# Attention pipeline on three shared PSUM banks, with the sums for the Strassen products of x and h moved from VectorE to GpSimd

## The chip, the cores and the metric

One core of a Trainium2 chip. The metric is the device time of one execution in microseconds (us), as the median of several runs. Engines: TensorE (PE in the profile, and PEld for its loading of weights), VectorE (DVE), ScalarE (ACT), GpSimd (POOL), and the queue that starts DMAs (SP).

## The reference

A transformer block on 2048 tokens of width 1024: a layer norm, linear attention with 32 heads of 32, a residual, a second layer norm, a gated ReLU MLP of width 3584, and a second residual.

```python
phi = lambda t: jnp.where(t > 0, t + 1, jnp.exp(t)) + 1e-6
pq, pk = phi(q), phi(k)
kv = jnp.einsum("bhsd,bhse->bhde", pk, v)
z = jnp.einsum("bhsd->bhd", pk)
num = jnp.einsum("bhqd,bhde->bhqe", pq, kv)
den = jnp.einsum("bhqd,bhd->bhq", pq, z)[..., None] + 1e-6
# ... o = num / den, put together again, times wo ...
h = x + _A_ref(_layernorm(x, axis=-1), A_wqkv, A_wo)
h2 = h + _B_ref(_layernorm(h, axis=-1), B_W_gate, B_W_up, B_W_down)
```

## The kernel before

The large products are made with Strassen's scheme in Winograd's form: seven products of quarters instead of eight, at the price of sums of quarters on both sides. The left sums are four additions or subtractions for each piece of the transposed, normalized x (`xT`) or h (`hnT`), all on VectorE. One of them is written over a quarter of its own input.

```python
def left_sums(T, S, cols):
    (a11, a12), (a21, a22) = [[v[:, :, cols] for v in row] for row in blocks(T)]
    s1, s2, s4 = (v[:, :, cols] for v in S)
    nc.vector.tensor_tensor(out=s1, in0=a21, in1=a22, op=ALU.add)
    nc.vector.tensor_tensor(out=s2, in0=s1, in1=a11, op=ALU.subtract)
    nc.vector.tensor_tensor(out=a21.bitcast(FP16), in0=a11, in1=a21, op=ALU.subtract)
    nc.vector.tensor_tensor(out=s4, in0=a12, in1=s2, op=ALU.subtract)
```

x is taken in four units of four tiles (128 tokens each). Unit 0 makes k and v with plain products, while units 1 to 3 are normalized, transposed and summed ahead of their Strassen products. Four x sums of 128x1024 belong to each unit.

```python
def ln_T(t):                                   # layer norm of a tile of x, then its transpose
    # ... bn_stats, bn_aggr on VectorE, ln and exp on ScalarE ...
    nc.vector.scalar_tensor_tensor(out=nmr, in0=mv[:, 0:1], scalar=-1.0, in1=rstd, op0=ALU.mult, op1=ALU.mult)
    nc.scalar.activation(out=xn[:], in_=x_sb[:], func=ACT.Identity, bias=nmr, scale=rstd)
    # ... DMA transpose into xT ...

def phi_end(dst, e):
    nc.scalar.activation(out=e, in_=dst, func=ACT.Exp, bias=negb[:, 0:1], scale=1.0)
    nc.vector.tensor_scalar(out=e, in0=e, scalar1=1.0, scalar2=PHI_EPS, op0=ALU.min, op1=ALU.add)
    nc.vector.tensor_tensor(out=dst, in0=dst, in1=e, op=ALU.max)

# ... in the loop over units: k products, kv of the unit before, v products ...
            for n, _ in enumerate(v_unit(u)):
                if n == 1 and u + 1 < NU:
                    sums_unit(u + 1)
        sums_unit(0)
```

In `strassen` ScalarE copies a product out of its bank (`snap`, tiles `m` and `u`), so that the next product may go on in that bank. VectorE evicts the finished products (`phi_begin` for k and q; the `v_sb` additions for v).

In the attention stage every tile passes four steps, each one step later than the one before: numerator and denominator (`nd`, one PSUM bank), the DMA transpose of the result (`oT`), the product with wo in two halves (`attn`, two other banks) with the layer norm of h, and the transpose of normalized h. The MLP's first products ("quads") fill TensorE in between. The sums of h are made in one piece of 128x2048 at the end of each half.

```python
abpool = abctx.enter_context(tc.tile_pool(name="abpool", bufs=2, space=PSUM, side="right"))
# ...
ndpool = abctx.enter_context(tc.tile_pool(name="ndpool", bufs=1, space=PSUM, side="right"))
# ...
LAG = (0, 1, 2, 3)
STS = ST // NS
QSTEPS = STS + 2
def attn_step(step):
    for k in range(4):
        n = step - LAG[k]
        if n in begin_at:
            n = begin_at.index(n)
            stages[n][k]()
            if k == 3 and (n + 1) % STS == 0:
                left_sums(hnT[n // STS], hns[n // STS], slice(0, SW))
```

Of the kernel before, what the change touches and what calls it, by code (L numbers as in the profile page):

```python
# [8 lines left out]
ALU = mybir.AluOpType  # L9
FP32 = mybir.dt.float32  # L10
BF16 = mybir.dt.bfloat16
FP16 = mybir.dt.float16
PSUM = bass.MemoryType.PSUM
# [18 lines left out]
def block_kernel(ctx: ExitStack, tc: tile.TileContext, x, wqkv, wo, wg, wu, wd, out, H: int):  # L32
    nc = tc.nc
    P = 128
    xf = x.flatten_outer_dims()
    of = out.flatten_outer_dims()
    S, D = xf.shape
# [4 lines left out]
    KC = D // P  # L42
    FC = F // P
    NW = 512
    NDW = P + HPC
    SW = 512
# [4 lines left out]
    NT = SW // P  # L51
# [20 lines left out]
    hh_dram = [[dram.tile([P, FH, SW], BF16, name=f"hh_dram{s}_{q}") for q in range(4)] for s in range(NS)]  # L72

    PE_T = 4
    XB, HB = 4, 2
    negb = consts.tile([P, 2], FP32, name="negb")
    nc.gpsimd.memset(negb[:, 0:1], -1.0 - PHI_EPS)
    nc.gpsimd.memset(negb[:, 1:2], 1.0 + PHI_EPS)
# [9 lines left out]
    bwork = pqctx.enter_context(tc.tile_pool(name="bwork", bufs=2, side="right"))  # L88
# [9 lines left out]
    xT, xS = [None] * NS, [None] * NS  # L98
# [5 lines left out]
    def blocks(T):  # L104
        return [[T[i][:, j * KH:(j + 1) * KH, :] for j in range(2)] for i in range(2)]

    def left_sums(T, S, cols):

        (a11, a12), (a21, a22) = [[v[:, :, cols] for v in row] for row in blocks(T)]
        s1, s2, s4 = (v[:, :, cols] for v in S)  # L110
        nc.vector.tensor_tensor(out=s1, in0=a21, in1=a22, op=ALU.add)
        nc.vector.tensor_tensor(out=s2, in0=s1, in1=a11, op=ALU.subtract)
        nc.vector.tensor_tensor(out=a21.bitcast(FP16), in0=a11, in1=a21, op=ALU.subtract)
        nc.vector.tensor_tensor(out=s4, in0=a12, in1=s2, op=ALU.subtract)

    def left_ops(T, S):
        (a11, a12), (a21, a22) = blocks(T)
# [83 lines left out]
    with ExitStack() as actx:  # L201
# [9 lines left out]
        x_tiles = {}  # L211

        def load_x(t):
            x_sb = bwork.tile([P, D], BF16, tag="x_res", bufs=XB, name="x_sb")
            nc.sync.dma_start(out=x_sb[:], in_=xf[t * P:(t + 1) * P, :])
            x_tiles[t] = x_sb

# [3 lines left out]
        def place(t):  # L221
            i, r = divmod(t * P, HS)
            s, r = divmod(r, SW)
            return s, i, r
# [3 lines left out]
        atiles = [t for u in units for t in u]  # L228
# [121 lines left out]

        def sums_unit(u):
            s, _, r = place(units[u][0])
            left_sums(xT[s], xS[s], slice(r, r + 2 * P))

        NU = len(units)

# [7 lines left out]
        for n, t in enumerate(units[0]):  # L364
            v_plain(t)
            if todo:
                ln_T(todo.pop(0))
            if n == 1:
                sums_unit(1)
                k_sums()  # L370
# [21 lines left out]
        for c in range(KC):  # L392
            bnk, i = divmod(c, GPB)
            nc.vector.tensor_tensor(out=kvz[:, c, :], in0=kv_ps[bnk][:, i * NDW:(i + 1) * NDW],
                                    in1=mask[:], op=ALU.mult)


    abctx = ExitStack()
    abpool = abctx.enter_context(tc.tile_pool(name="abpool", bufs=2, space=PSUM, side="right"))
    qw = []  # L400

    def q_unit(s, c):
# [26 lines left out]


    mctx = ExitStack()
    ndpool = abctx.enter_context(tc.tile_pool(name="ndpool", bufs=1, space=PSUM, side="right"))

    hnT, hns = [], []

# [24 lines left out]
    def attn_stages(t):  # L460

        i, r = divmod(t * P, HS)
        s, r = divmod(r, SW)
        st = {}

        def nd():
            o_sb = bwork.tile([P, D], BF16, tag="o_sb", name="o_sb")
            st["o"] = o_sb
            ov = o_sb[:].rearrange("p (k h e) -> p k h e", k=KC, h=HPC)
            for c0, n in pieces:  # L470
                ps = ndpool.tile([P, NW], FP32, tag="nd", name="nd")
                for c in range(c0, c0 + n):
                    nc.tensor.matmul(ps[:, (c - c0) * NDW:(c - c0 + 1) * NDW], lhsT=pqT[:, c, t * P:(t + 1) * P],
                                     rhs=kvz[:, c, :], start=True, stop=True)
                ndv = ps[:, 0:n * NDW].rearrange("p (k w) -> p k w", w=NDW)
                den = bsmall.tile([P, GPB, HPC], FP32, tag="den", name="den")
                nc.scalar.activation(out=den[:, 0:n], in_=ndv[:, :, P:NDW], func=ACT.Identity, bias=deps[:], scale=1.0)
                rd = bsmall.tile([P, GPB, HPC], FP32, tag="rd", name="rd")
                nc.vector.reciprocal(out=rd[:, 0:n], in_=den[:, 0:n])
                nc.vector.tensor_tensor(  # L480
                    out=ov[:, c0:c0 + n], in0=ndv[:, :, 0:P].rearrange("p k (h e) -> p k h e", h=HPC),
                    in1=rd[:, 0:n, :].unsqueeze(3).to_broadcast([P, n, HPC, Dh]), op=ALU.mult)

        def oT():
            st["oT"] = bwork.tile([P, KC, P], BF16, tag="oT", name="oT")
            nc.sync.dma_start_transpose(out=st["oT"][:], in_=st["o"][:])
            x_sb = bwork.tile([P, D], BF16, tag="x_res", bufs=XB, name="x_res")
            nc.sync.dma_start(out=x_sb[:], in_=xf[t * P:(t + 1) * P, :])
            st["x"] = x_sb

        def wo_h():
            h_sb = st["x"]
            tot = bsmall.tile([P, 2], FP32, tag="tot", name="tot")
            for j in range(2):
                ps = abpool.tile([P, NW], FP32, tag="ab", name="attn")
                for c in range(KC):
                    nc.tensor.matmul(ps[:], lhsT=st["oT"][:, c, :], rhs=wo_sb[:, c, j * NW:(j + 1) * NW],  # L497
                                     start=(c == 0), stop=(c == KC - 1))
                nc.vector.scalar_tensor_tensor(out=h_sb[:, j * NW:(j + 1) * NW], in0=ps[:], scalar=1.0,  # L499
                                               in1=h_sb[:, j * NW:(j + 1) * NW], op0=ALU.mult, op1=ALU.add,  # L500
                                               accum_out=tot[:, j:j + 1])
            nc.sync.dma_start(out=h_dram[t][:], in_=h_sb[:])
            st["hn"] = bwork.tile([P, D], BF16, tag="hn", bufs=HB, name="hn")

            sm = bsmall.tile([P, 6], FP32, tag="sm", name="sm")
            nmean, var, lnv, rstd, nmr = (sm[:, i:i + 1] for i in range(5))
            nc.vector.tensor_tensor(out=nmean, in0=tot[:, 0:1], in1=tot[:, 1:2], op=ALU.add)
            nc.vector.tensor_scalar(out=nmean, in0=nmean, scalar1=-1.0 / D, scalar2=None, op0=ALU.mult)
            nc.scalar.activation(out=st["hn"][:], in_=h_sb[:], func=ACT.Square, bias=nmean, scale=1.0, accum_out=var)
            nc.scalar.activation(out=lnv, in_=var, func=ACT.Ln, bias=LN_EPS, scale=1.0 / D)  # L510
            nc.scalar.activation(out=rstd, in_=lnv, func=ACT.Exp, scale=-0.5)
            nc.vector.tensor_tensor(out=nmr, in0=nmean, in1=rstd, op=ALU.mult)
            nc.scalar.activation(out=st["hn"][:], in_=h_sb[:], func=ACT.Identity, bias=nmr, scale=rstd)

        def hn_T():
            nc.sync.dma_start_transpose(out=hnT[s][i][:, :, r:r + P], in_=st["hn"][:])

        return nd, oT, wo_h, hn_T

    LAG = (0, 1, 2, 3)  # L520
    STS = ST // NS
    QSTEPS = STS + 2
    stages = [attn_stages(t) for t in order]
    begin_at = [n if n < STS else n - STS + QSTEPS for n in range(ST)]

    def attn_step(step):
        for k in range(4):
            n = step - LAG[k]
            if n in begin_at:
                n = begin_at.index(n)  # L530
                stages[n][k]()
                if k == 3 and (n + 1) % STS == 0:
                    left_sums(hnT[n // STS], hns[n // STS], slice(0, SW))

    rest = [p for s in range(1, NS) for c in range(0, KH, 2) for p in [q_unit(s, c)] * 6]
    for step in range(QSTEPS):
        attn_step(step)
        for p in rest[step * len(rest) // QSTEPS:(step + 1) * len(rest) // QSTEPS]:
            next(p)
# [123 lines left out]
    for f in range(NE):  # L663
        st = {}
# [3 lines left out]
            next(st["q"])  # L668

        flow += [begin] + [lambda st=st: next(st["q"])] * 5  # L670
    ready = STS + LAG[3]
    for step in range(QSTEPS, ready):
        if step == QSTEPS:
            flow.pop(0)()
        attn_step(step)
    steps = QSTEPS + STS + LAG[3] - ready
    for n in range(steps):
        attn_step(ready + n)
        for p in flow[n * len(flow) // steps:(n + 1) * len(flow) // steps]:
# [13 lines left out]
    prev, k = None, 1  # L693
# [129 lines left out]
@with_exitstack  # L823
def kernel(
    ctx: ExitStack,
    tc: tile.TileContext,
    A_x: bass.AP,
    A_wqkv: bass.AP,
    A_wo: bass.AP,
    B_x: bass.AP,  # L830
    B_W_gate: bass.AP,
    B_W_up: bass.AP,
    B_W_down: bass.AP,
    out: bass.AP,
):
    block_kernel(tc, A_x, A_wqkv, A_wo, B_W_gate, B_W_up, B_W_down, out, H=32)
# [30 lines left out]
```

## Time and profile before

776.76 us, median of 3 runs (773.99 to 778.0). The profiled run has a span of 773.6 us at a mean granted TensorE clock of 0.996.

The first part of the page gives the busy time of every engine, its share of the span and its instructions.

```profile
PE 742.8 (96%) x3584; PEld 337.9 (44%) x3584; DVE 490.0 (63%) x924; ACT 313.6 (41%) x529; POOL 3.5 (0%) x34
```

TensorE is the limit and GpSimd does nothing. The table of windows cuts the span at events of TensorE. The columns are the window, its length, the busy time (and instructions) of PE, PEld, DVE, ACT and POOL, the granted clock, the share of DMA and GB/s. The first row shown is from the first Strassen product of k to that of the second unit; the second is from the first quad to the first wide quad (where attention is over).

```profile
40.62:70.53 29.91, 26.86 (x145) 12.80 (x144) 29.21 (x56) 23.26 (x39) 0.50 (x4) 1.00 0.59 127
...
208.58:301.44 92.86, 88.30 (x433) 39.50 (x432) 69.31 (x200) 52.83 (x114) 0.00 (x0) 0.96 0.54 124
```

In the first of these VectorE is busy for 29.21 of 29.91 us. It is the crowded place that the change wants to relieve. The waits of TensorE (total, times, longest) name what is lost to whom:

```profile
PE attn L497 <- DMA oT<-o_sb: 5.8, 7, 2.5
...
PE Aq L276 <- ACT v_sb L329: 1.1, 1, 1.1
...
PE Aq L276 <- ACT m L143: 0.7, 2, 0.5
```

### The profile page before, as it was taken

The numbers are of one execution on the slowest core, as the hardware profiler recorded it, in microseconds if no ns is written. First come the engines' busy times: TensorE is split into PE (matmuls) and PEld (weight loads), VectorE is DVE, ScalarE is ACT, GpSimd is POOL, SyncE is SP. The second block draws the span as 40 slices with busy tenths as digits, with TensorE's granted clock in tenths as the row PEclk, the third lists the DMA queues.
The fourth block names the chain that finished last, engine by engine and source line by source line (L and its number), as shares of the span: only waits on it lengthen the run. The fifth ranks groups of instructions, "written<-read, shape, count | busy, mean of one in ns | idle before, by whom it ended". The sixth has DMA issues, their size and how long they took to land.

```text
span 773.6 us, 9575 instructions
## 1 busy us (share of the span) xinstructions
PE 742.8 (96%) x3584; PEld 337.9 (44%) x3584; DVE 490.0 (63%) x924; ACT 313.6 (41%) x529; POOL 3.5 (0%) x34
## 2 busy tenths in 40 slices
PE   5989999989979998999999999999999999999998
PEld 2444555434434443444444444444443444444443
DVE  6998545876878767675464654646554991349732
ACT  4775554856836654444444444444443000000000
POOL 0000000000000000000000000000000000000000
PEclk9999999999989999999999999999999999999999
DMA  9863003097656545354014040140001985971001
GB/s 311 235 134 82 0 1 109 2 244 175 154 108 149 137 109 144 116 157 136 7 37 121 28 136 8 34 123 28 27 8 40 310 283 193 308 286 48 28 27 55
DMA packets 125150, 89.76 MB, mean 116 GB/s; under 512 B 50352, under 2 KB 116912, under 8 KB 124592
## 3 DMA queue, kind: packets, MB, share of 16 engines
q1 hardware_dynamic: 125104, 89.15, 40.6%
q8 instruction: 28, 0.46, 0.2%
q14 instruction: 18, 0.15, 0.1%
HBM read 59.77 MB, written 17.83 MB: 100 GB/s over the span
## 4 chain that ended last, share of the span: by engine, by line
PE 44%; DVE 11%; ACT 3%; issue 2%; DMA 1%; DVEq 0%
PE A L576 15%; PE accA L737 10%; PE E L576 8%; PE accE L737 6%; DVE gu L595 4%; PE Dp L576 3%; ACT snap L590 2%; PE accD L737 2%; DVE hh L598 1%; DMA out_dram<-o 1%; ACT gu L597 1%; DVE hh L651 1%; DVE tg L559 1%; DVE tu L556 1%; DVE tg L556 1%
## 5 line engine op out<-in xcount | busy, mean ns | idle before, releaser
L595 DVE TENSOR_TENSOR gu<-E,snap 128x1024 bf16<-128x1024 f32 x48 | 58.7, 1222 | 88.1 <-ACT snap L590 85.5
L590 ACT COPY snap<-A 128x1024 f32<-128x1024 f32 x72 | 72.0, 1008 | 85.6 <-PE A L576 85.6
L737 PEld LDWEIGHTS <-hh 128*128 128x128 bf16 (+1 forms) x560 | 54.7, 98 | 67.7 <-issue 1.9
L597 ACT ACTIVATE gu<-gu 128x512 bf16<-128x512 bf16 x72 | 45.4, 630 | 86.7 <-DVE gu L595 86.4
L737 PE MATMUL accA<-wd,hh 128*128 128x512 f16 (+1 forms) x336 | 73.3, 379 | 1.4 <-DVE gu L595 1.4
L497 PE MATMUL attn<-wo_mem,oT 128*128 128x512 bf16 x256 | 62.9, 388 | 5.8 <-DMA oT<-o_sb 5.8
L576 PEld LDWEIGHTS <-tg 128*128 128x128 f16 x384 | 37.5, 98 | 50.8 <-issue 6.8
L576 PEld LDWEIGHTS <-tu 128*128 128x128 f16 x384 | 37.6, 98 | 45.3
L598 DVE TENSOR_TENSOR hh<-gu 128x512 bf16<-128x512 bf16 x72 | 30.4, 423 | 38.1 <-ACT gu L597 38.1
L576 PE MATMUL A<-hn,tg 128*128 128x512 f16 (+1 forms) x192 | 49.3, 379 | 1.1 <-ACT snap L590 1.1
L576 PE MATMUL A<-hn,tu 128*128 128x512 f16 (+1 forms) x192 | 49.3, 379 | 0.0
L143 ACT COPY u<-Aq 128x512 f32<-128x512 f32 x56 | 32.0, 581 | 29.2 <-PE Aq L276 19.1
L576 PEld LDWEIGHTS <-wg 128*128 128x128 bf16 x288 | 28.1, 98 | 35.6 <-issue 2.4
L576 PEld LDWEIGHTS <-wu 128*128 128x128 bf16 x288 | 28.2, 98 | 34.0
L497 PEld LDWEIGHTS <-oT 128*128 128x128 bf16 x256 | 24.1, 99 | 32.7 <-DMA oT<-o_sb 8.4
L737 PEld LDWEIGHTS <-s 128*128 128x128 f16 x224 | 21.9, 98 | 27.2 <-issue 0.8
L595 DVE TENSOR_TENSOR gu<-Dp,snap 128x1024 bf16<-128x1024 f32 x24 | 29.3, 1219 | 1.9 <-PE Dp L576 1.9
L276 PEld LDWEIGHTS <-xT 128*128 128x128 bf16 (+1 forms) x192 | 18.6, 98 | 24.8 <-issue 3.1
L745 DVE TENSOR_TENSOR u<-accA,hres 128x512 f32<-128x512 f32 x16 | 10.7, 687 | 28.4 <-PE accA L737 27.9
L480 DVE TENSOR_TENSOR o_sb<-nd,rd 128x384 bf16<-128x384 f32 (+1 forms) x48 | 24.5, 510 | 4.3 <-DMA oT<-o_sb 2.1
L499 DVE SCALAR_TENSOR_TENSOR x_res<-attn,x_res 128x512 bf16<-128x512 f32 x32 | 21.9, 684 | 7.0 <-PE attn L497 6.6
L576 PE MATMUL A<-hs,tg 128*128 128x512 f16 x96 | 24.6, 379 | 1.1 <-ACT snap L590 1.1
(159 smaller groups left out, 1216.8 us busy)
## 6 DMA issues: line engine op xcount, KB each, us to landing
wd<-in_B_W_down_dram SPq DMA_DIRECT2D x16, 896.0 KB, 6.9
hh_dram<-hh SPq DMA_DIRECT2D x72, 128.0 KB, 1.7
wg<-in_B_W_gate_dram SPq DMA_DIRECT2D x14, 512.0 KB, 5.1
wu<-in_B_W_up_dram SPq DMA_DIRECT2D x14, 512.0 KB, 6.1
hh<-hh_dram SPq DMA_DIRECT2D x4, 1792.0 KB, 8.8
x_sb<-in_A_x_dram SPq DMA_DIRECT2D x16, 256.0 KB, 3.2
x_res<-in_A_x_dram SPq DMA_DIRECT2D x16, 256.0 KB, 2.9
h_dram<-x_res SPq DMA_DIRECT2D x16, 256.0 KB, 2.4
```

The lines of the kernel that those rows point to most:

```text
L143: nc.scalar.copy(out=snaps[nm, v], in_=A[v][:])
L276: nc.tensor.matmul(ps[:], lhsT=left[m - 1][:, kc, r + v * P:r + (v + 1) * P], rhs=right[m - 1][:, kc, :], start=(start and kc == 0), stop= ...
L480: nc.vector.tensor_tensor(out=ov[:, c0:c0 + n], in0=ndv[:, :, 0:P].rearrange("p k (h e) -> p k h e", h=HPC), in1=rd[:, 0:n, :].unsqueeze(3 ...
L497: nc.tensor.matmul(ps[:], lhsT=st["oT"][:, c, :], rhs=wo_sb[:, c, j * NW:(j + 1) * NW], start=(c == 0), stop=(c == KC - 1))
L499: nc.vector.scalar_tensor_tensor(out=h_sb[:, j * NW:(j + 1) * NW], in0=ps[:], scalar=1.0, in1=h_sb[:, j * NW:(j + 1) * NW], op0=ALU.mult, ...
L556: nc.vector.tensor_tensor(out=t[:, 0], in0=b[0][1], in1=b[0][0], op=ALU.subtract)
L576: nc.tensor.matmul(ps[:, v, :], lhsT=w[v][m - 1][:, kc, :], rhs=left[m - 1][:, kc, :], start=(start and kc == 0), stop=(kc == KH - 1), ski ...
L590: nc.scalar.copy(out=m[:], in_=ps[:])
L595: nc.vector.tensor_tensor(out=gu[:], in0=ps[:], in1=m[:], op=ALU.add)
L597: nc.scalar.activation(out=gu[:, 0, :], in_=gu[:, 0, :], func=ACT.Relu)
L598: nc.vector.tensor_tensor(out=d, in0=gu[:, 0, :], in1=gu[:, 1, :], op=ALU.mult)
L737: nc.tensor.matmul(accs[tt][:], lhsT=lhs[:, half * FD + f, tt * P:(tt + 1) * P], rhs=rhs[half][:, f, :], start=(start and half == 0 and f ...
```

## The change

Two things are done at once. The attention stage gets one pool of three banks for `nd` and `attn` together, three buffers for `oT`, other lags and two steps fewer before the second half starts; the sums of h are made in slices of one tile. And the left sums of x and of h go to GpSimd, to take 20.7 us of work off VectorE (16 sums of 0.68 us and 8 of 1.22 us).

```diff
-    def left_sums(T, S, cols):
+    def left_sums(T, S, cols, eng):
-        nc.vector.tensor_tensor(out=s1, in0=a21, in1=a22, op=ALU.add)
+        eng.tensor_tensor(out=s1, in0=a21, in1=a22, op=ALU.add)
 (... the other three sums likewise ...)
-            left_sums(xT[s], xS[s], slice(r, r + 2 * P))
+            left_sums(xT[s], xS[s], slice(r, r + 2 * P), nc.gpsimd)
-    abpool = abctx.enter_context(tc.tile_pool(name="abpool", bufs=2, space=PSUM, side="right"))
+    abpool = abctx.enter_context(tc.tile_pool(name="abpool", bufs=3, space=PSUM, side="right"))
-    ndpool = abctx.enter_context(tc.tile_pool(name="ndpool", bufs=1, space=PSUM, side="right"))
+    ndpool = abpool
 (... x tiles: three buffers of each of two tags, was four of one; oT shares one of these tags; x is read again in a stage of its own, x_in ...)
-    LAG = (0, 1, 2, 3)
+    LAG = (0, 1, 1, 2, 4)
-    QSTEPS = STS + 2
+    QSTEPS = STS + 0
-                if k == 3 and (n + 1) % STS == 0:
-                    left_sums(hnT[n // STS], hns[n // STS], slice(0, SW))
+                if k == len(LAG) - 1 and n % STS >= NT:
+                    left_sums(hnT[n // STS], hns[n // STS], slice(n % NT * P, (n % NT + 1) * P), nc.gpsimd)
```

More of the change, by code (lines that the diff above doesn't have):

```diff
@@ L74, in block_kernel @@
     PE_T = 4
-    XB, HB = 4, 2
+    XB, HB = 3, 2
     negb = consts.tile([P, 2], FP32, name="negb")
@@ L105, in blocks @@
         return [[T[i][:, j * KH:(j + 1) * KH, :] for j in range(2)] for i in range(2)]
-    def left_sums(T, S, cols):
+    def left_sums(T, S, cols, eng):
         (a11, a12), (a21, a22) = [[v[:, :, cols] for v in row] for row in blocks(T)]
         s1, s2, s4 = (v[:, :, cols] for v in S)
-        nc.vector.tensor_tensor(out=s1, in0=a21, in1=a22, op=ALU.add)
-        nc.vector.tensor_tensor(out=s2, in0=s1, in1=a11, op=ALU.subtract)
-        nc.vector.tensor_tensor(out=a21.bitcast(FP16), in0=a11, in1=a21, op=ALU.subtract)
-        nc.vector.tensor_tensor(out=s4, in0=a12, in1=s2, op=ALU.subtract)
+        eng.tensor_tensor(out=s1, in0=a21, in1=a22, op=ALU.add)
+        eng.tensor_tensor(out=s2, in0=s1, in1=a11, op=ALU.subtract)
+        eng.tensor_tensor(out=a21.bitcast(FP16), in0=a11, in1=a21, op=ALU.subtract)
+        eng.tensor_tensor(out=s4, in0=a12, in1=s2, op=ALU.subtract)
     def left_ops(T, S):
@@ L213, in load_x @@
         def load_x(t):
-            x_sb = bwork.tile([P, D], BF16, tag="x_res", bufs=XB, name="x_sb")
+            x_sb = bwork.tile([P, D], BF16, tag=("x_res", "oT")[atiles.index(t) % 2], bufs=XB, name="x_sb")
             nc.sync.dma_start(out=x_sb[:], in_=xf[t * P:(t + 1) * P, :])
@@ L470, in nd @@
             for c0, n in pieces:
-                ps = ndpool.tile([P, NW], FP32, tag="nd", name="nd")
+                ps = ndpool.tile([P, NW], FP32, tag="ab", name="nd")
                 for c in range(c0, c0 + n):
@@ L484, in oT, with x_in @@
         def oT():
-            st["oT"] = bwork.tile([P, KC, P], BF16, tag="oT", name="oT")
-            nc.sync.dma_start_transpose(out=st["oT"][:], in_=st["o"][:])
+            oT = bwork.tile([P, D], BF16, tag="oT", bufs=XB, name="oT")
+            st["oT"] = oT[:].rearrange("p (c t) -> p c t", c=KC)
+            nc.sync.dma_start_transpose(out=st["oT"], in_=st["o"][:])
+        def x_in():
             x_sb = bwork.tile([P, D], BF16, tag="x_res", bufs=XB, name="x_res")
@@ L516, in hn_T @@
             nc.sync.dma_start_transpose(out=hnT[s][i][:, :, r:r + P], in_=st["hn"][:])
-        return nd, oT, wo_h, hn_T
-    LAG = (0, 1, 2, 3)
+        return nd, oT, x_in, wo_h, hn_T
+    LAG = (0, 1, 1, 2, 4)
     STS = ST // NS
-    QSTEPS = STS + 2
+    QSTEPS = STS + 0
     stages = [attn_stages(t) for t in order]
@@ L526, in attn_step @@
     def attn_step(step):
-        for k in range(4):
+        for k in range(len(LAG)):
             n = step - LAG[k]
@@ L670, in block_kernel @@
         flow += [begin] + [lambda st=st: next(st["q"])] * 5
-    ready = STS + LAG[3]
+    ready = STS + LAG[-1]
     for step in range(QSTEPS, ready):
@@ L675, in block_kernel @@
         attn_step(step)
-    steps = QSTEPS + STS + LAG[3] - ready
+    steps = QSTEPS + STS + LAG[-1] - ready
     for n in range(steps):
```

## The prediction

> **What bounds the kernel now.** TensorE. The page's busy table gives PE 742.8 of 773.6 us (96%). Counting matmuls at their spacing in the timeline (0.216 us for 512 columns, 0.058 for 132) the work is about 728 us, so about 45 us of the span is not matmul issue. From about 305 us the chain of waits is TensorE with small vector pieces, and the change doesn't touch that code. What can be won lies before 305 us. By the busy table in 10-us windows, TensorE is idle there 23 us: about 8.5 at the start, 3 between 40 and 70 us, 9.5 between 150 and 230 us, 2 at 300-310 us. Between 220 and 230 us the granted clock is also only 0.66, after 2.6 idle us in the window before; that costs 2-3 us more. Named waits in the attention stage (waits of PE): oT transposes 5.8 us, Dq on vector evictions 2.4 us, nd on its single bank 1.0 us; weight loads for nd waited 11.8 us for o_sb. VectorE is 90-100% busy from 10 to 70 us and 66-98% from 150 to 220 us.
>
> **What the change does.** The counts of TensorE work stay the same. nd and attn share three banks instead of one plus two; oT has three buffers; the second half starts two steps earlier (20 steps, not 21); a tile's nd matmuls and its 16 attn matmuls now stand together in the order. Hn transposes come one step later. VectorE loses 16 sums of 128x1024 (0.68 us each, 10.9 us) and 8 of 128x2048 (1.22 us each, 9.8 us). GpSimd gets 16 of 128x1024 and 32 of 128x512. The trace has no such GpSimd operation; the Trainium skill, "GPSIMD Engine Reference", Performance versus the Vector engine, gives about 2.6 cycles per element, so my estimate is 2.2 and 1.2 us: about 36 us for x, 38 us for h.
>
> The cost: "SBUF — State Buffer", Who interferes with whom, says a GpSimd instruction that reads SBUF and a vector instruction with two SBUF inputs lock each other out whole. The weight sums (1.2 us each; tv around 35-45 us, tq around 52-60 us) and the phi maximum fall in the same stretches, so a vector instruction will wait up to 2.2 us, and the evictions queued behind it too.
>
> **On the critical path.**
> - 40-70 us: the kv matmuls move into a hole, but tv sums collide with the sums of unit 1; S2 still arrives near 42-44 us. Loss 3 us becomes 3-7: +2.
> - 150-230 us: fewer bank waits and fewer steps, -5; the clock dip may vanish, -2; against it, in the pure-attention steps the first attn bank waits for nd's eviction (1.2 us), and the first S2 product waits for the late transpose plus two GpSimd sums (about 3 us, as large as the wait that VectorE makes now): +2. The oT wait behind the gate/up loads (2.5 us) stays.
> - 300-310 us: the sums of h are sliced and early, -1.
>
> Sum: -4 us.
>
> **Predicted: 772.5 us, 80% range 763 to 782.** Faster by over 2%: 0.08; within 2%: 0.83; slower by over 2%: 0.09.
>
> **What would show it.** GpSimd busy near 75-80 us; sums of 2.2 and 1.2 us; vector two-input sums stretched over 1.22 and 0.68 us at 35-75 us; TensorE idle of 150-230 us down from 9.5 to about 5 us; nd waits for o_sb gone; the windows after 310 us unchanged in length.
>
> **What would make it wrong.** If GpSimd and VectorE hardly block each other, or the attention stage gets nearly gapless at full clock: 760-765 us. If blocked vector evictions stall TensorE through 40-75 us and again beside the h sums, or the late h sums hold the first quads: 780-790 us.

## More of the kernel before

Last, some groups of VectorE instructions up to 306 us (line, operation, output from input, shapes, count; then busy us and the mean ns of one; then idle time before them). The first line is the statistics of the layer norm of x, the 128x1 line the small product in it, the two 128x1024 lines are the end of phi, and the 128x2048 one is a weight sum.

```profile
L245 DVE BATCH_NORM_STATS2 stats<-x_sb 128x6 f32<-128x512 bf16 x32 | 21.0, 672 | 6.6 <-DMA x_sb<-in_A_x_dram 6.6
...
L191 DVE TENSOR_TENSOR wo_mem<-wo_mem,e 128x1024 bf16<-128x1024 bf16 x12 | 8.2, 687 | 0.2
L190 DVE TENSOR_SCALAR e<-e 128x1024 bf16<-128x1024 bf16 x12 | 5.0, 420 | 0.4 <-ACT e L189 0.2
...
L253 DVE SCALAR_TENSOR_TENSOR sma<-mv,sma 128x1 f32<-128x1 f32 x16 | 2.3, 151 | 0.8 <-ACT sma L251 0.7
L129 DVE TENSOR_TENSOR wq_sb<-wq_sb 128x2048 f16<-128x2048 bf16 x1 | 1.2, 1217 | 0.0
```

## The result, and the profile after

803.27 us, median of 4 runs (803.07 to 803.42), against 776.88 us (773.99 to 778.0, 4 runs) for the kernel before on the same chip. The ratio is 1.0345, with a 95% interval of 1.0317 to 1.0374: 3.4% slower. (Here and below, a ratio is the mean time of one kernel's runs over that of the other's runs of the same rounds, so it is not quite the ratio of the medians quoted.) The prediction was 772.5 us, within 763 to 782: it was wrong.

The page of the profile after, span 801.3 us, mean clock 0.976:

```profile
PE 751.4 (94%) x3525; PEld 342.8 (43%) x3584; DVE 501.3 (63%) x900; ACT 313.7 (39%) x529; POOL 82.7 (10%) x82
```

VectorE has 24 instructions fewer and is busy for 11 us longer. That is the finding in one line: the work was taken away, and what stayed got slower by more than was taken. The windows between the same events as before:

```profile
43.09:92.81 49.72, 34.06 (x144) 14.52 (x145) 43.06 (x46) 24.22 (x40) 34.28 (x17) 0.79 0.28 63
...
227.71:331.71 104.00, 93.22 (x442) 42.23 (x449) 77.35 (x206) 56.16 (x119) 37.38 (x32) 0.95 0.54 133
```

All stretches, in us:

| from TensorE's event to its next | before | after | difference |
|---|---|---|---|
| start to first Strassen product of k | 40.62 | 43.09 | +2.5 |
| to that of the second unit | 29.91 | 49.72 | +19.8 |
| to the first product of q | 54.15 | 54.14 | 0.0 |
| to the first attn | 46.59 | 47.03 | +0.4 |
| to the first quad | 37.31 | 33.73 | -3.6 |
| to the first wide quad | 92.86 | 104.00 | +11.1 |
| to the end | 472.16 | 469.59 | -2.6 |
| sum | 773.60 | 801.30 | +27.7 |

The rows "to the first quad" and "to the first wide quad" belong together: work was moved from one to the other. All the loss is where GpSimd is busy (34.28 and 37.38 us in the two rows shown above), and the stretch between them, where GpSimd rests, is unchanged. The waits of TensorE after:

```profile
PE Aq L276 <- ACT m L143: 8.1, 3, 3.8
...
PE attn L500 <- DVE o_sb L480: 3.8, 5, 1.5
PE Aq L276 <- ACT v_sb L329: 3.5, 1, 3.5
PE attn L500 <- DMA oT<-o_sb: 3.4, 1, 3.4
PE attn L500 <- DVE rd L479: 3.0, 2, 2.7
```

The first wait is said to be for ScalarE, whose busy time did not change. The VectorE groups up to 345 us show what is behind it:

```profile
L245 DVE BATCH_NORM_STATS2 stats<-x_sb 128x6 f32<-128x512 bf16 x32 | 20.8, 669 | 5.5 <-DMA x_sb<-in_A_x_dram 5.5
...
L191 DVE TENSOR_TENSOR wo_mem<-wo_mem,e 128x1024 bf16<-128x1024 bf16 x12 | 11.8, 987 | 0.3
...
L190 DVE TENSOR_SCALAR e<-e 128x1024 bf16<-128x1024 bf16 x12 | 10.5, 875 | 0.3 <-ACT e L189 0.3
L253 DVE SCALAR_TENSOR_TENSOR sma<-mv,sma 128x1 f32<-128x1 f32 x16 | 9.9, 626 | 0.8 <-ACT sma L251 0.7
...
L129 DVE TENSOR_TENSOR wq_sb<-wq_sb 128x2048 f16<-128x2048 bf16 x1 | 3.1, 3139 | 0.0
```

The statistics with one input keep their speed (0.672 us before). The maximum at the end of phi goes from 0.687 to 0.987 us, the `tensor_scalar` before it from 0.420 to 0.875, one weight sum from 1.217 to 3.139, and the 128x1 product, the smallest instruction of all, from 0.151 to 0.626.

Now one passage in order of time. These are the timelines of GpSimd, VectorE, ScalarE and TensorE of the kernel after, in this order, near 76 us (start us, duration us, engine, line, operation, output from input; in brackets the idle time before it and what ended it):

```profile
74.44 2.18 POOL L112 TENSOR_TENSOR xS<-xS,xT 128x1024 f16<-128x1024 f16 x1
76.58 2.56 POOL L113 TENSOR_TENSOR xT<-xT,xT 128x1024 f16<-128x1024 bf16 x1
79.10 2.30 POOL L114 TENSOR_TENSOR xS<-xT,xS 128x1024 f16<-128x1024 bf16 x1
```

```profile
74.67 2.48 DVE L191 TENSOR_TENSOR wo_mem<-wo_mem,e 128x1024 bf16<-128x1024 bf16 x1
77.08 2.34 DVE L190 TENSOR_SCALAR e<-e 128x1024 bf16<-128x1024 bf16 x1
79.45 2.49 DVE L191 TENSOR_TENSOR wo_mem<-wo_mem,e 128x1024 bf16<-128x1024 bf16 x1
81.87 0.41 DVE L190 TENSOR_SCALAR e<-e 128x1024 bf16<-128x1024 bf16 x1
```

```profile
77.19 1.15 ACT L189 ACTIVATE e<-wo_mem,negb 128x1024 bf16<-128x1024 bf16 x1 [3.22 <-DVE wo_mem L191]
78.25 0.57 ACT L143 COPY m<-Aq 128x512 f32<-128x512 f32 x1
```

```profile
78.86 1.86 PE L276 MATMUL Aq<-tv,xS 128*128 128x512 f16 x4 [3.82 <-ACT m L143]
```

Read it from the top. The VectorE instruction at 74.67 began after the GpSimd sum at 74.44, and ended at 77.15: about when that sum was over (76.62) and its own 0.68 us were spent. The next ones at 77.08 and 79.45 each wait in the same way for the GpSimd sum that had started before them, and the one at 81.87, with no sum left, takes 0.41 us again. ScalarE waited 3.22 us for VectorE; the copy of `m` stood behind that in its queue; and TensorE waited 3.82 us for the copy. Then the four matmuls took 1.86 us instead of 1.02. That is the granted clock: the window table gives 1.00 between 40 and 100 us before, and after 0.81, 0.67 and 0.64 in the slices of 40-50, 50-60 and 80-90 us. The Trainium skill, "TensorE: Matmul & The Clock Gate", What's actually happening, says that the array's clock falls to half after an idle stretch; the trace agrees in this place, with 1.86 us for four matmuls after 3.82 us of waiting and 1.02 us for four at full clock.

### The profile page after: what moved, and what is told of

Same layout as the page of the kernel before. It is cut to its first block, busy times and chain, and to the rows that moved or that the text cites. A ratio compares the mean times of both kernels' runs of the same rounds, so it can differ in the third digit from the quotient of the medians. Undisturbed runs are those within 1.5% of the kernel's fastest.

```text
span 801.3 us, 9569 instructions
## 1 busy us (share of the span) xinstructions
PE 751.4 (94%) x3525; PEld 342.8 (43%) x3584; DVE 501.3 (63%) x900; ACT 313.7 (39%) x529; POOL 82.7 (10%) x82
## 4 chain that ended last, share of the span: by engine, by line
PE 46%; DVE 11%; ACT 3%; issue 2%; DVEq 0%
PE A L579 15%; PE accA L740 11%; PE E L579 8%; PE accE L740 6%; DVE gu L598 4%; PE Dp L579 3%; ACT snap L593 2%; PE accD L740 2%; PE Aq L612 1%; DVE hh L601 1%; PE Eq L612 1%; ACT gu L600 1%; DVE hh L654 1%; DVE tg L562 1%; DVE tu L559 1%
## 5 line engine op out<-in xcount | busy, mean ns | idle before, releaser
L500 PEld LDWEIGHTS <-oT 128*128 128x128 bf16 x256 | 25.5, 103 | 47.0 <-issue 19.4
L276 PEld LDWEIGHTS <-xS 128*128 128x128 f16 x144 | 15.2, 105 | 30.6 <-issue 16.4
L189 ACT ACTIVATE e<-pq_mem,negb 128x512 bf16<-128x512 bf16 x32 | 22.7, 720 | 10.5 <-DVE pq_mem L184 10.4
```

Of the source, the lines that this page charges most:

```text
L276: nc.tensor.matmul(ps[:], lhsT=left[m - 1][:, kc, r + v * P:r + (v + 1) * P], rhs=right[m - 1][:, kc, :], start=(start and kc == 0), stop= ...
L500: nc.tensor.matmul(ps[:], lhsT=st["oT"][:, c, :], rhs=wo_sb[:, c, j * NW:(j + 1) * NW], start=(c == 0), stop=(c == KC - 1))
```

## The experiments

The theory (A): a GpSimd instruction that reads SBUF and a VectorE instruction that needs the interface they share lock each other out, each for its whole length. The Trainium skill states it in "SBUF — State Buffer", Who interferes with whom: a VectorE instruction with two SBUF inputs meets GpSimd's reads, one in a two-port mode (a 16-bit `tensor_scalar` can be) meets GpSimd at all, and "Whoever issues first gets the shared pair for the whole instruction". What locked instructions hold up behind them is the time lost. (The texts call this `tensor_scalar` "4x": in the profile before it takes 0.289 us for 128x512 and 0.420 for 128x1024, so 0.13 us for 512 columns more, a quarter of the 0.53 by which an eviction from PSUM grows, 0.688 to 1.221.) The first rival (B): the new buffers of x and the new order. The second (C): GpSimd is slow (2.12 us against 0.68 us for a sum), so the results come late and TensorE waits for them. A third (D): only the tiny 128x1 instructions matter, as they stand in the latency chain of the layer norms.

Medians with lowest, highest and count; ratio to the kernel before, of the same rounds:

| run | what it is | us | ratio (95%) |
|---|---|---|---|
| after | the change | 803.27 (803.07-803.42, 4) | 1.0345 (1.0317-1.0374) |
| x_vec | after, x sums on VectorE | 777.74 (775.73-779.35, 4) | 1.0011 (0.9974-1.0047) |
| h_vec | after, h sums on VectorE | 793.20 (791.35-795.25, 4) | 1.0219 (1.0185-1.0253) |
| xh_vec | after, both on VectorE | 771.44 (769.21-772.92, 4) | 0.9936 (0.9902-0.9969) |
| b_x_pool | before, x sums on GpSimd | 790.86 (790.21-791.11, 4) | 1.0187 (1.0159-1.0215) |
| xh_dummy | xh_vec, 32 idle additions beside the x sums | 789.66 (788.59-791.68, 4) | 1.0169 (1.0142-1.0197) |
| x_write_only | after, x sums replaced by writes | 779.27 (778.45-780.73, 4) | 1.0035 (1.0009-1.0060) |
| xvec_ptr | x_vec, 128x1 instructions rewritten | 778.03 (773.93-780.09, 4) | 1.0005 (0.9961-1.0049) |
| xh_ptr | xh_vec, the same rewriting | 773.64 (772.72-774.87, 4) | 0.9961 (0.9937-0.9985) |
| xh_dummy_late | xh_vec, 32 idle additions after the x sums | 778.32 (776.18-780.46, 4) | 1.0027 (1.0003-1.0050) |
| unit0_late | xh_vec, the x sums of unit 0 on GpSimd, late | 770.15 (769.87-774.39, 6) | 0.9931 (0.9910-0.9952) |
| h_whole | xh_vec, h sums in one piece | 771.05 (769.25-772.69, 6) | 0.9934 (0.9914-0.9954) |
| h_dummy | xh_vec, 32 idle additions beside the h sums | 790.14 (786.78-792.95, 6) | 1.0169 (1.0145-1.0192) |

The kernel before had medians from 775.42 to 777.67 us in these batches. Every kernel but x_write_only gave correct results.

### Taking the change apart: x_vec, h_vec, xh_vec, b_x_pool

```diff
 x_vec, against after
-            left_sums(xT[s], xS[s], slice(r, r + 2 * P), nc.gpsimd)
+            left_sums(xT[s], xS[s], slice(r, r + 2 * P), nc.vector)
 h_vec, against after
-                    left_sums(hnT[n // STS], hns[n // STS], slice(n % NT * P, (n % NT + 1) * P), nc.gpsimd)
+                    left_sums(hnT[n // STS], hns[n // STS], slice(n % NT * P, (n % NT + 1) * P), nc.vector)
 xh_vec: both of these
 b_x_pool, against before
-            left_sums(xT[s], xS[s], slice(r, r + 2 * P))
+            left_sums(xT[s], xS[s], slice(r, r + 2 * P), nc.gpsimd)
```

> The changed kernel with the sums of x back on VectorE, the sums of h still on GpSimd. Theory A (the sums of x on GpSimd lock VectorE out and cost the 20-22 us that the changed kernel loses before its 95th microsecond): 779 to 783 us, second k unit starting near 70-72 us instead of 92.8. Rival B (the loss in the head comes from the new x buffers and the new order of the three-bank pipeline): 797 to 803 us, second k unit still near 90 us.

> The changed kernel with the sums of h (still in slices) on VectorE, the sums of x on GpSimd. If the 7 us more overhead in the stage of the first quads come from GpSimd's lock and latency: 793 to 796 us. If they come from the three-bank pipeline itself: 800 to 805 us (VectorE gets 13 us more work there).

> Three-bank pipeline alone, all sums on VectorE. Theory A: 771 to 776 us, as fast as the kernel before or a little faster, because only GpSimd did harm. Rival B: 795 us or more. Mixed (the pipeline itself loses some us in the stage of the first quads): 777 to 783 us.

> The kernel before with only the sums of x moved to GpSimd. Theory A: 795 to 801 us, vector operations with two SBUF inputs and the 4x tensor_scalar stretched at 23-85 us as in the changed kernel. Rival B: 774 to 779 us.

From xh_vec on: the x sums on GpSimd cost 21.8 us (to h_vec), the h sums 6.3 (to x_vec), both together 31.8 (to after, which was timed in another batch). So the x sums cost 21.8 to 25.5 us and the h sums 6.3 to 10.1, depending on whether the other is there. The same move of the x sums in the kernel before, with its own buffers and order, costs 15.4 us (790.86 against the 775.42 us of before in that batch). That misses the 795 to 801 us expected; x_vec, too, came out a little below its 779 to 783. Theory B falls as the cause: the new pipeline on its own does not lose, it is 0.64% faster than the kernel before, a little outside the noise. But it makes the x sums dearer. In b_x_pool the sums of unit 3 start at 80.7 us, when the burst at the end of phi is over (69.8 to 75.4 us, its instructions at their old 0.42 and 0.69 us); in h_vec they start at 72.2 us, in the middle of that burst. TensorE begins the second unit at 84.2 us in b_x_pool and at 93.6 us in h_vec.

### Does it need a late result? xh_dummy and x_write_only

xh_dummy leaves all sums on VectorE and lets GpSimd make additions whose result nobody reads. The order of the instructions on all other engines is the same as in xh_vec.

```diff
 xh_dummy, against xh_vec
+    idle = consts.tile([P, 2, 2 * P], FP16, name="idle")
         def sums_unit(u):
             s, _, r = place(units[u][0])
+            (a11, a12), (_, a22) = [[v[:, :, r:r + 2 * P] for v in row] for row in blocks(xT[s])]
+            for p, q in ((a11, a22), (a12, a22), (a11, a12), (a12, a11)):
+                for k in range(0, KH, 2):
+                    nc.gpsimd.tensor_tensor(out=idle[:], in0=p[:, k:k + 2], in1=q[:, k:k + 2], op=ALU.add)
             left_sums(xT[s], xS[s], slice(r, r + 2 * P), nc.vector)
```

> The three-bank pipeline with all sums on VectorE, plus 32 additions of 128x512 on GpSimd that read normalized x from SBUF and write a scratch tile that nobody reads; the orders of TensorE, VectorE, ScalarE and of the DMA queue are the same, instruction for instruction, as without them. If GpSimd's reads lock VectorE out, this alone costs 10 to 25 us: 781 to 797 us. If the changed kernel lost its time because results of GpSimd came late (a 2.1 us operation in place of 0.68 us), nothing here comes late: 769 to 774 us.

It takes 18 us more than xh_vec (1.0169 against 0.9936), though the profile names no wait for these additions. (VectorE's own x sums ran into them, 18.4 us in all instead of 10.9, so the 18 us show that reads alone cost time and not how much the change lost by them.) x_write_only goes the other way. It is the kernel after, with the same dependencies on GpSimd, but every x sum is replaced by a subtraction of 4 columns, which keeps the waits, and two fills of the whole output, which keep GpSimd busy without reading. Its results are wrong (relative error 0.82), and the order on PE, DVE, ACT and SP is that of after.

```diff
 x_write_only, against after
+    def left_blanks(T, S, cols):
+        (... a11 to a22, s1, s2, s4 as in left_sums ...)
+        s3 = a21.bitcast(FP16)
+        for o, p, q in ((s1, a21, a22), (s2, s1, a11), (s3, a11, a21), (s4, a12, s2)):
+            nc.gpsimd.tensor_tensor(out=o[:, :, 0:1], in0=p[:, :, 0:1], in1=q[:, :, 0:1], op=ALU.subtract)
+            nc.gpsimd.memset(o, 0.0)
+            nc.gpsimd.memset(o, 0.0)
-            left_sums(xT[s], xS[s], slice(r, r + 2 * P), nc.gpsimd)
+            left_blanks(xT[s], xS[s], slice(r, r + 2 * P))
```

> The changed kernel in which each sum of x on GpSimd is replaced by a four-column subtraction and two memsets of the whole output (result wrong on purpose); same order of all other engines, same dependencies, GpSimd about as long busy[...], but nearly no reads of SBUF by GpSimd. If the reads lock VectorE out: 777 to 785 us, the 128x1 and two-input vector operations back at their old durations, the 4x tensor_scalar perhaps still stretched. If lateness of GpSimd's results is the cause: 797 to 806 us.

779.27 us: 24 us less than after, and within the noise of x_vec. Between 40 and 70 us GpSimd is busy for 28.30 us (26.05 in after), yet TensorE is busy for 26.66 us at a clock of 1.00 (22.30 at 0.83 in after). The results come as late: the sums of unit 1 take 12.2 us from the first start to the last end in both runs, and one VectorE instruction waited 2.5 us for a fill. So a result on GpSimd as late as this does not hurt; theory C falls for x. The list of waits of after agrees: of the waits of other engines for a GpSimd result it names one, of 0.3 us. The groups of VectorE up to 110 us in x_write_only (lines are ten later than in after) show a difference between the kinds:

```profile
L201 DVE TENSOR_TENSOR wo_mem<-wo_mem,e 128x1024 bf16<-128x1024 bf16 x8 | 5.5, 687 | 0.2
L200 DVE TENSOR_SCALAR e<-e 128x1024 bf16<-128x1024 bf16 x8 | 5.4, 678 | 0.7 <-ACT e L199 0.7
...
L263 DVE SCALAR_TENSOR_TENSOR sma<-mv,sma 128x1 f32<-128x1 f32 x16 | 2.3, 151 | 0.8 <-ACT sma L261 0.7
```

The two instructions with two inputs are back at 0.687 and 0.151 us, just as before: pure writes don't hold them. The `tensor_scalar` stays lengthened, 0.678 against 0.420 us: it is held by writes too. Both agree with the page cited.

### Is it only the tiny instructions? xvec_ptr and xh_ptr

```diff
 xvec_ptr, against x_vec; xh_ptr, against xh_vec
-            nc.vector.scalar_tensor_tensor(out=nmr, in0=mv[:, 0:1], scalar=-1.0, in1=rstd, op0=ALU.mult, op1=ALU.mult)
+            nc.vector.tensor_scalar(out=nmr, in0=mv[:, 0:1], scalar1=rstd, scalar2=-1.0, op0=ALU.mult, op1=ALU.mult)
-            nc.vector.tensor_tensor(out=nmean, in0=tot[:, 0:1], in1=tot[:, 1:2], op=ALU.add)
+            nc.vector.tensor_scalar(out=nmean, in0=tot[:, 0:1], scalar1=tot[:, 1:2], scalar2=None, op0=ALU.add)
-            nc.vector.tensor_tensor(out=nmr, in0=nmean, in1=rstd, op=ALU.mult)
+            nc.vector.tensor_scalar(out=nmr, in0=nmean, scalar1=rstd, scalar2=None, op0=ALU.mult)
```

> Sums of x on VectorE, sums of h on GpSimd, and the three 128x1 vector operations of the layer norms rewritten so that they have one SBUF tensor input and a per-partition scalar. If the way of the 6 us that the sums of h cost goes through these tiny operations being locked out for up to 1.2 us each, with ScalarE waiting for them in order and TensorE for ScalarE: 770 to 774 us, and they last 0.15 us. If it goes through the larger two-input operations: 776 to 780 us.

> Control: all sums on VectorE with the same rewriting of the three 128x1 operations. There is no lock to avoid, so 769 to 773 us, the same as without the rewriting; a change of over 3 us would mean that the rewriting itself, or the new order that it leads to, does something.

The second input becomes one value for each partition. The Trainium skill, "DVE: scalar operands, raw-bit mode, write accounting and state across instructions", Scalar operands, says that such an operand takes no second stream, and the trace agrees: beside GpSimd's sums of h these instructions take 0.198 and 0.210 us, and 0.198 and 0.207 in the control without GpSimd. But the time is 778.03 against 777.74 us: nothing was won. Larger instructions are locked with and without the rewriting: the gated product takes 0.504 us (0.581 in x_vec, 0.422 in the control), and three kinds of weight sum of 128x512 take 0.553 to 0.557 us (0.418 to 0.421 in x_vec, where another kind took 0.596). This is not a clean removal. The rewriting let the scheduler order TensorE, VectorE and ScalarE differently, and the control itself came out at 773.64 us, above its 769 to 773. Against the control the h sums cost 0.44% of the time of before, against xh_vec 0.75%, and the intervals are as wide as the difference: what share of the h sums' cost goes through the tiny instructions stays open. For the x sums the tiny ones are not all: in the passage at 74 to 82 us ScalarE waited for instructions of 128x1024.

### Where the h sums lose: x_vec beside xh_vec, and h_dummy

In x_vec only the h sums are on GpSimd. At 208 us the first of them has just begun, so nothing can yet wait for it. The timelines of GpSimd, VectorE and TensorE in x_vec:

```profile
208.02 1.33 POOL L111 TENSOR_TENSOR hs<-hn 128x512 f16<-128x512 bf16 x1 [97.35 <-DMA hn<-hn]
```

```profile
208.39 0.97 DVE L515 TENSOR_TENSOR sm<-sm 128x1 f32<-128x1 f32 x1
209.29 0.41 DVE L562 TENSOR_TENSOR tu<-wu,tu 128x512 f16<-128x512 bf16 x1
209.62 0.54 DVE L480 TENSOR_TENSOR o_sb<-nd,rd 128x384 bf16<-128x384 f32 x1
```

```profile
210.31 4.89 PE L500 MATMUL attn<-wo_mem,oT 128*128 128x512 bf16 x16 [2.69 <-DVE rd L479]
```

And the same two instructions, VectorE's and TensorE's, in xh_vec:

```profile
206.58 0.10 DVE L515 TENSOR_TENSOR sm<-sm 128x1 f32<-128x1 f32 x1
```

```profile
207.63 3.61 PE L500 MATMUL attn<-wo_mem,oT 128*128 128x512 bf16 x16 [1.81 <-DVE rd L479]
```

A product of one number for each partition took 0.97 us instead of 0.10. Behind it stood the eviction that TensorE needed. The wait grew by 0.88 us, and then 16 matmuls took 1.28 us longer at the lower clock: 2.2 us from one locked instruction. There are two more such places. At 228 us the waits around one tile grow by 0.3 us and its matmuls by 1.7. At 278 us a 128x1 addition takes 1.07 us, ScalarE's square waits for it, the copy of `m` stands behind the square, and TensorE waits 2.34 us more and loses 1.6 us of clock over the next eight matmuls. (The locked addition accounts for 0.9 us of this wait; how the rest arose was not taken apart.) Together 8.1 us. The two profiled runs are further apart than the medians, 777.6 and 767.1 us of span, and 1.8 us of that lie before the first quad, where no h sum has started. By the stage, from the first quad to the first wide quad, the profiles agree: 95.2 us in xh_vec and 95.1 in h_vec, with the h sums on VectorE, 103.9 in x_vec and 104.0 in after, with them on GpSimd. And the profile of x_vec names no wait of another engine for a sum of GpSimd.

h_dummy was meant to show the same with idle additions, as xh_dummy did for x.

```diff
 h_dummy, against xh_vec
+    idle = consts.tile([P, KH, P], FP16, name="idle")
                 if k == len(LAG) - 1 and n % STS >= NT:
+                    cols = slice(n % NT * P, (n % NT + 1) * P)
+                    (a11, a12), (_, a22) = [[v[:, :, cols] for v in row] for row in blocks(hnT[n // STS])]
+                    for p, q in ((a11, a22), (a12, a22), (a11, a12), (a12, a11)):
+                        nc.gpsimd.tensor_tensor(out=idle[:], in0=p, in1=q, op=ALU.add)
```

> The three-bank pipeline with all sums on the vector engine (771.4 us, 0.9936), plus 32 GpSimd additions of 128x512 that stand where the sums of h stood on GpSimd, read the same quarters of hn and write a scratch tile that nobody reads; the order of all other engines is unchanged. If the sums of h cost 6 to 10 us because GpSimd's reads lock vector instructions out (theory), this costs about as much though nothing waits for the additions: 776 to 782 us, ratio 1.000 to 1.009, and the 128x1 additions of the layer norm of h again lengthen to about 1 us where they meet an addition. If the cost of the sums of h came from their results being late (four sums of 1.15 us in a row on GpSimd against 0.42 us each on the vector engine, with the first quads waiting; rival), this stays at 771 to 773 us, ratio 0.993 to 0.996. In between would mean both.

790.14 us is beyond what was expected, and for another reason: the 128x1 instructions lengthened little (0.147 to 0.195 and 0.250 us), but VectorE's own sums of h start on the same transpose as the additions and ran into them. The 32 sums took 28.3 us instead of 13.4 (8 times the four means). So it shows again that GpSimd's reads alone cost time there, with no result awaited, but the run is harsher than the change and gives no size for it. That the cost of the h sums in x_vec is the lock rests on the three places in its trace, of which the first is the clean one, and on the absence of waits for GpSimd.

### Can it be put where VectorE has room? xh_dummy_late and unit0_late

```diff
 xh_dummy_late, against xh_vec
             left_sums(xT[s], xS[s], slice(r, r + 2 * P), nc.vector)
+            if u == NU - 1:
+                p, _, q = (v[:, :, r:r + 2 * P] for v in xS[s])
+                for k in range(32):
+                    k = k % 2 * 2
+                    nc.gpsimd.tensor_tensor(out=idle[:], in0=p[:, k:k + 2], in1=q[:, k:k + 2], op=ALU.add)
 unit0_late, against xh_vec: the x sums of unit 0, not needed before q, wait for the last sums of unit 3
+            if u == 0:
+                nc.gpsimd.tensor_copy(out=xS[s][0][:, :, r:r + 1], in_=xS[1][2][:, :, SW - 1:SW])
-            left_sums(xT[s], xS[s], slice(r, r + 2 * P), nc.vector)
+            left_sums(xT[s], xS[s], slice(r, r + 2 * P), nc.vector if u else nc.gpsimd)
```

> The same 32 dummy additions of 128x512 on GpSimd as in the run with dummies, now behind the last sums of x (they read those), so between about 74 and 115 us, where VectorE is busy 40 to 70% and TensorE isn't waiting for it; orders of the other engines unchanged. The lock exists here too (two-input and 4x vector operations of that stretch are lengthened, up to 1.2 us each), but VectorE has slack: 770 to 775 us, against the 18 us that the same dummies cost early. If GpSimd's reads cost TensorE time wherever they stand: 782 to 792 us.

> Three-bank pipeline, all sums on VectorE except those of the first x unit, which nobody needs before 124 us; GpSimd does them after the last sums of x, at about 74 to 83 us. VectorE is relieved of 2.7 us in or just behind its full stretch, TensorE lost 2.7 us there in all: 769 to 772 us, at best 1 to 2 us faster than all sums on VectorE; over 775 us would mean that the lock bites there too.

In the kernel before VectorE is busy for only 16.79 us between 70 and 100 us, so 32 additions there were expected to cost nothing. They cost about 7 us (1.0027 against 0.9936): a miss. The VectorE timeline of xh_dummy_late shows why, first while the additions run and then, in the next unit, when they are over:

```profile
86.79 1.37 DVE L191 TENSOR_SCALAR e<-e 128x1024 bf16<-128x1024 bf16 x1
88.19 1.52 DVE L192 TENSOR_TENSOR wo_mem<-wo_mem,e 128x1024 bf16<-128x1024 bf16 x1
...
118.61 0.42 DVE L191 TENSOR_SCALAR e<-e 128x1024 bf16<-128x1024 bf16 x1
119.06 0.69 DVE L192 TENSOR_TENSOR wo_mem<-wo_mem,e 128x1024 bf16<-128x1024 bf16 x1
```

The work of VectorE comes in a burst there: four such pairs, with the eviction of the next product behind them in its queue. Three of the four took about 2.9 us instead of 1.1, and TensorE waited 1.87 and 2.76 us. Room on average was no room at that moment. In unit0_late a tiny copy, which reads the end of the last sum of unit 3, keeps the sums of unit 0 back, because the scheduler otherwise puts them first. With these four sums the cost is nothing, and so is the gain: 770.15 us.

### Is the slicing of the h sums the gain? h_whole

```diff
 h_whole, against xh_vec
-                if k == len(LAG) - 1 and n % STS >= NT:
-                    left_sums(hnT[n // STS], hns[n // STS], slice(n % NT * P, (n % NT + 1) * P), nc.vector)
+                if k == len(LAG) - 1 and (n + 1) % STS == 0:
+                    left_sums(hnT[n // STS], hns[n // STS], slice(0, SW), nc.vector)
```

> Three-bank pipeline, all sums on VectorE, the sums of h in one piece of 128x2048 behind the last transpose, as in the kernel before. Slicing costs VectorE 3.6 us more in instructions (8 x 4 x 0.42 against 2 x 4 x 1.22) but lets the sums start early. If the pipeline's small gain comes from the early slices: 774 to 778 us. If it comes from banks and steps: 768 to 772 us.

0.9934 beside 0.9936 for xh_vec: no. In xh_vec the wide quads start at 297.41 us (301.44 before), and the rest takes 469.7 us (472.2 before); which part of the pipeline gives how much was not taken apart further. The best version found is xh_vec, the three-bank pipeline with all sums on VectorE, at 771.44 us; unit0_late and h_whole are equal to it within the noise.

## Why the prediction was wrong

- "GpSimd busy near 75-80 us; sums of 2.2 and 1.2 us": nearly right. 82.7 us, as the lock stretched the x sums too (about 42 us in all, not 36); a sum of 128x1024 takes 2.12 us when undisturbed and one of 128x512 1.15 us. The figure used, about 2.6 cycles for an element (the Trainium skill, "GPSIMD Engine Reference", Performance versus the Vector engine), gives an estimate of 2.2 us at the 1.2 GHz of its Specifications.
- "lock each other out whole": right in mechanism, and the stretched instructions were seen at 35-75 us as foretold.
- "40-70 us: ... Loss 3 us becomes 3-7: +2": this is the step that failed. The term was measured at +22.3 us (2.5 up to the first Strassen product of k, and 19.8 from there to the next unit). Three things were left out of it. First, each collision was priced alone ("up to 2.2 us") and no total was made. From the trace before, 12.5 us of VectorE work between 40 and 70 us, besides the x sums themselves, is of the kinds that lock: weight sums 7.2 us, the end of phi 4.4, the 128x1 products 0.9. The sums of units 1 to 3, which stood between 37 and 64 us, are 12 times 2.12, or 25.4 us, on GpSimd. By this estimate 38 us of exclusive demand stand in some 30 us. It could have been made beforehand, with the predicted 2.2 us for a sum, and would have spoken against +2, though it does not give the 22.3. Second, the `tensor_scalar` of phi and the tiny 128x1 products were not seen as lockable, and they were stretched most (by 5.5 and 7.6 us in all). Third, the prediction named the evictions queued behind a locked instruction, but not how the delay goes on: through ScalarE's queue to TensorE, as at 74 to 82 us, and then again in clock, which was 0.79 on average from 43 to 93 us.
- "150-230 us: ... -5; the clock dip may vanish, -2; against it ... +2": the pipeline alone is worth about 5 us in all, as xh_vec shows, and the nd weight loads' wait for o_sb went from 11.8 to 0.3 us as foretold. The sum was right rather than the places: in the profiles of before and xh_vec, 3.2 of 6.5 us were won between the first attn and the first wide quad, and TensorE's idle time from 150 to 230 us fell from 9.5 to 8.7 us, not to 5. In after the dip did not vanish, and the sums of h cost 6.3 to 10.1 us; in the places looked at it was tiny instructions, locked in front of an eviction or of ScalarE. The prediction's +2 was for late results in this stage, not for the lock.
- "300-310 us: ... -1": the rest of the kernel became 2.6 us shorter. That the slices made it so is not borne out by h_whole, whose time is the same.
- "The oT wait behind the gate/up loads (2.5 us) stays": right, 3.4 us.
- What would make it wrong, "If blocked vector evictions stall TensorE through 40-75 us and again beside the h sums ... 780-790": the case that came true, but larger. The evictions, which read PSUM and one SBUF tile, were not locked themselves and kept their 0.69 us; they stood behind locked instructions.

## What to carry to other kernels

Before two-input work goes to GpSimd, add up in each stage how long GpSimd will hold the shared interface and how long VectorE needs it for two-input instructions, however small, and for `tensor_scalar` on 16-bit tiles: here 38 us in some 30 us would have warned of the loss, which VectorE's share of 63% over the span does not show. If the sum fits, look still at how VectorE's work is bunched and what stands behind it: here the delay was passed on to whoever waited for its evictions, and the same x sums cost 15.4 us in the kernel before and 21.8 in the new pipeline. To tell a lock from a late result, let GpSimd do idle reads that nobody awaits, or writes in place of reads with the waits kept, and see which one keeps the time.

## What the Trainium skill lacked or had wrong

- "SBUF — State Buffer", Who interferes with whom, gives the rule and no size for small instructions. The runs show that a 128x1 instruction with two inputs, of 0.10 to 0.15 us, is held as long as a large one: 0.97 and 1.07 us beside a GpSimd sum of 128x512, and a mean of 0.626 us for 16 of them beside sums of 128x1024. It agrees in all else that was tried, also that pure writes hold a `tensor_scalar` (0.678 us against 0.420) and not an instruction with two inputs (0.687, 0.687).
- "GPSIMD Engine Reference", Engine selection, calls GpSimd about 2 times slower for two inputs; here, on 16-bit tiles, it was 3.1 times for 128x1024 (2.12 against 0.68 us).
- "TensorE: Matmul & The Clock Gate", What's actually happening, sets the fall to half clock after an idle window of about 3.4 us. Here shorter waits were enough: in x_vec four matmuls took 1.86 us instead of 1.03 after a single wait of 2.34 us, and 16 took 4.89 us instead of 3.61 after one of 2.69 us.
- No page gives the duration of a GpSimd fill: 128x1024 of 16 bits took 0.95 us.
